# A gated MLP's last group in one phase of 512 tokens, with late products put off and TensorE's order written out

## The chip, the cores and the metric

One core of a Trainium2 chip runs the whole program. The time is the device time of one execution, in microseconds; the kernel before has a median of 612.99 us over 3 runs (610.72 to 613.15). The profile is of one execution, whose own time is 612.58 us and whose span, from the first to the last instruction, is 610.9 us. Engines are called as the profile calls them: PE is TensorE, PEld its weight loads, DVE is VectorE, ACT is ScalarE, POOL is GpSimd, SP issues most transfers.

## The reference

The program is three layers one after the other, on 1536 tokens of width 512, all in float32:

```
attn:  q, k, v (2, 8, 768, 64): each query sees the first 4 keys and the 128 keys up to its own; softmax
x    = attn with the heads side by side                       # (1536, 512)
mlp:   g = x @ w_gate;  x = (g / (1 + exp(-g)) * (x @ w_val)) @ w_out      # 512 -> 1536 -> 512
moe:   tokens with x @ w_skip > 0 are computed, the others are copied
       e = argmax(x @ w_gate2);  p = softmax(x @ w_gate2)[e]               # 8 experts
       out = x + p * (relu(x @ w1[e]) @ w2[e])                             # 512 -> 1024 -> 512
```

## The kernel before

Products that need more than TensorE's reduced float32 are split: a value is a rounded part and a rest (`hi` and `lo`, or `hh` and `hl`), and a product is three matmuls, hi by hi, hi by lo and lo by hi. ACT rounds (`act_copy`, line 71), and DVE or POOL takes the rest (`lo_of`, line 74).

Tokens go in 12 blocks of 128, three groups of four. Attention of a group runs between the MLP work of the group before. `PHASES` (line 38) lists the MLP's phases: group 0 and group 1 in one phase of 512 tokens each, group 2 in two phases of 256 tokens. A phase goes over the hidden layer in 12 chunks of 128. For each chunk `mlp` (line 571) projects to the gate and to the value (`proj`, 12 matmuls each, line 547), makes `th`, `hh` and `hl` on ACT and DVE, and then calls `down` (line 559) for the chunk before: three matmuls of 512 columns for each tile of 128 tokens, added up in a PSUM bank per tile (`acc`). The chunk's weights are split on the way (`prep`) into a ring of 12 buffers, anew in every phase.

After a group comes its routing. `take` copies a tile out of PSUM to `x2`, `turn` transposes it on PE (`x2t`, line 680), `logits` multiplies it by the gate weights (`lp`, line 688), and `choose` finds the expert and the row that each token gets in the buffer `xs` (small DVE operations, and the matmuls `rp` of lines 721 to 724), and scatters the rows there by indirect DMA from POOL's queue. For the groups listed in `APART` the gate sums come another way: `weigh` (line 692) multiplies a tile by one row of the gate weights on DVE, 36 times for a group, and `finish_apart` hands them out during the next phase. Before, this is group 0 alone.

`finish_last` ends the last phase. The tokens of expert 0 that were scattered before are loaded from `xs` as `xg`, and those of the last two tiles are put to them on PE, with one-hot matrices `at` (`start_x`, `put_in`, line 902), so that the first expert need not wait for the last scatter. Then `experts` goes over the 8 experts. An expert has a first block of 128 rows and, if it has more, a second of up to 64, under a branch: `block_h` and `few_h` (first layer, `hps`, lines 993 and 949), `turn_x` (transposes `xg`, line 934), `block_turn` and `few_turn` (transpose the hidden layer, `htp`), `block_y` and `few_y` (second layer, `yps`, lines 1019 and 975). `prep2` loads an expert's weights in pieces of four through 11 buffers called `stage` and splits them: ACT all four, POOL one rest, DVE three (`w<-stage,w` at line 74). `load_x` fetches an expert's rows when they have landed.

Each engine works its instructions off in the order in which they stand, one after the other. A scheduler puts them in that order when the program is built, on every engine, by the priority of the code's order and by what it takes to be ready.

Of the kernel before, what the change touches and what calls it, by code (L numbers as in the profile page):

```python
# [8 lines left out]
F32 = mybir.dt.float32  # L9
# [6 lines left out]
P = 128  # L16

@with_exitstack
def build(ctx: ExitStack, tc: tile.TileContext, q, k, v, n_sink, window,
# [53 lines left out]
    def lo_of(out, in_, hi, eng=None):  # L73
        (eng or nc.vector).tensor_tensor(out=out, in0=in_, in1=hi.bitcast(F32), op=ALU.subtract)  # L74
# [448 lines left out]
    LO = ["gvo", "", "", ""]  # L523
# [13 lines left out]
    hp = {}  # L537
    acc = {}
# [12 lines left out]
    def down(g, c, tiles, base=0):  # L551
        whi, wlo = wr["o", c]
        hh, hl = hp[c]
        for t in tiles:
# [3 lines left out]
            for m, (h_, w_) in enumerate(((hh, whi), (hh, wlo), (hl, whi))):  # L558
                nc.tensor.matmul(out=acc[g, t], lhsT=h_[:, s], rhs=w_, start=c == 0 and m == 0, stop=c == NFC - 1 and m == 2)  # L559
# [10 lines left out]

    def mlp(ph):
        g, t0, t1, c0, c1, _ = PHASES[ph]
        n = (t1 - t0) * P
        for c in range(c0, c1 + 1):
            if c < c1:
# [9 lines left out]
                act_copy(hh, th, 0.5)  # L585
                nc.vector.scalar_tensor_tensor(out=hl, in0=th, scalar=0.5, in1=hh.bitcast(F32), op0=ALU.mult, op1=ALU.subtract)  # L586
                hp[c] = (hh, hl)
                pace(ph, c)
# [71 lines left out]
    def route(pools, toks, rows, apart=None):  # L660
# [8 lines left out]
        def take(t, src):  # L669
            x2 = mo_.tile([P, RW], F32, tag="x2", name="x2", bufs=4)  # L670
            act_copy(x2[:, 0:DM], src)
# [5 lines left out]
        def turn(t):  # L677
# [4 lines left out]
            nc.vector.tensor_copy(x2T, tp)  # L682
# [12 lines left out]
        return take, turn, logits if apart is None else weigh, lambda meanwhile=None: choose(rt_, pa_ if apart is None else ps_, n, lp, [x2s[t] for t in range(n)], meanwhile)  # L695

    def choose(rt_, ps_, n, lp, x2s, meanwhile=None):
# [20 lines left out]
        if meanwhile:  # L718
            meanwhile[0]()
# [10 lines left out]
        if meanwhile:  # L730
            meanwhile[1](x2s, po)
# [97 lines left out]
    def finish_last(g, tiles, late):  # L829

        take, turn, logits, close = routing(g, tiles)
        n = len(tiles)
        a, b = NFC - 2, NFC - 1
        for c in (a, b):
            down(g, c, tiles[:-1], tiles[0])
        for i in range(n - 1):
            take(i, acc[g, tiles[i]])
        down(g, a, tiles[-1:], tiles[0])
# [531 lines left out]
```

## Time and profile before

| | |
|---|---|
| median of 3 runs | 612.99 us (610.72 to 613.15) |
| profiled execution | 612.58 us, span 610.9 us |
| PE busy | 578.4 us, 95% of the span, 3385 matmuls |
| DVE busy | 461.0 us, 75% |
| ACT busy | 369.3 us, 60% |
| POOL busy | 211.4 us, 35% |
| granted PE clock, mean | 0.979 of full speed |

PE's busy time is modelled for matmuls that overlap, so the distance from one matmul to the next says more than the duration of one. Times within the span are counted from its start. The last group's two phases begin at 331.17 us, the first expert's `hps` at 453.53 us, and the last matmul ends at 599.62 us.

### The profile page before, as it was taken

What the parts mean: (1) busy time and instruction counts of PE and PEld (TensorE: products, weight loads), DVE (VectorE), ACT (ScalarE), POOL (GpSimd) and SP (SyncE); (2) the same over time, 40 slices, a digit from 0 to 9 for tenths busy, and PEclk for the clock granted to TensorE, in tenths of its full rate; (3) what the DMA queues carried; (4) which work ended last, traced back from release to release, by engine and by line L of the source; (5) the groups of instructions that cost most, each with busy time, mean ns of one, the idle gap of its engine ahead of it and who ended that gap; (6) DMA issues with size and microseconds to landing.
All of it is one profiled execution on the core that took longest, in us unless ns stands there. A gap on an engine that the chain in (4) does not pass through costs nothing. (4 is left out here: it accounts for less than half of the span.)

```text
span 610.9 us, 10856 instructions
## 1 busy us (share of the span) xinstructions
PE 578.4 (95%) x3385; PEld 460.0 (75%) x3385; DVE 461.0 (75%) x1160; ACT 369.3 (60%) x864; POOL 211.4 (35%) x291
## 2 busy tenths in 40 slices
PE   7999999899999999999999999999997999999992
PEld 4556766677777777778788999889985787777771
DVE  4898898897657999976645676699657887988950
ACT  4888787876555664555543565575444766857720
POOL 3474362656543342322320300021034335545320
PEclk7999999899999999999999999999997999999997
DMA  8857889563212422000016000032029776969701
GB/s 200 216 141 182 235 248 257 167 208 57 83 16 35 131 38 67 12 19 1 17 44 217 30 1 0 35 116 70 1 79 324 248 242 210 344 205 307 279 7 33
DMA packets 89305, 78.22 MB, mean 128 GB/s; under 512 B 53371, under 2 KB 65659, under 8 KB 89234
## 3 DMA queue, kind: packets, MB, share of 16 engines
q1 hardware_dynamic: 86434, 71.71, 39.6%
q0 software_dynamic: 2512, 5.68, 2.8%
q8 instruction: 31, 0.51, 0.4%
q14 instruction: 40, 0.33, 0.2%
q10 hardware_dynamic: 288, 0.00, 0.0%
HBM read 67.73 MB, written 12.00 MB: 131 GB/s over the span
## 5 line engine op out<-in xcount | busy, mean ns | idle before, releaser
L547 PE MATMUL gv<-xt,ring 128*128 128x512 f32 (+1 forms) x1152 | 224.2, 345 | 0.9 <-DVE th L581 0.9
L547 PEld LDWEIGHTS gv<-xt,ring 128*128 128x128 f32 x1152 | 177.3, 189 | 28.8 <-issue 2.0
L71 ACT ACTIVATE ring<-w 128x512 fp32r<-128x512 f32 x144 | 90.1, 628 | 92.7 <-PE gv L547 70.0
L74 DVE TENSOR_TENSOR ring<-w,ring 128x512 fp32r<-128x512 f32 x108 | 75.3, 699 | 33.2 <-ACT ring L71 33.1
L74 DVE TENSOR_TENSOR w<-stage,w 128x512 fp32r<-128x512 f32 x96 | 88.7, 955 | 7.0 <-ACT w L71 4.1
L559 PE MATMUL acc<-ring,hh 128*128 128x512 f32 x288 | 92.5, 402 | 0.0
L71 ACT ACTIVATE w<-stage 128x512 fp32r<-128x512 f32 x128 | 73.1, 626 | 11.8 <-DMA stage<-in_moe_w_dram 9.0
L74 POOL TENSOR_TENSOR ring<-w,ring 128x512 fp32r<-128x512 f32 x36 | 49.2, 1368 | 52.2 <-ACT ring L71 47.8
L74 POOL TENSOR_TENSOR w<-stage,w 128x512 fp32r<-128x512 f32 x32 | 47.1, 1476 | 46.6 <-ACT w L71 23.6
L559 PEld LDWEIGHTS acc<-ring,hh 128*128 128x128 f32 x288 | 50.8, 188 | 11.5 <-issue 1.2
L559 PE MATMUL acc<-ring,hl 128*128 128x512 f32 x144 | 57.1, 398 | 0.0
L1019 PE MATMUL yps<-w,hT 128*128 128x512 f32 x192 | 47.1, 399 | 1.0 <-DVE w L74 0.6
L394 POOL TENSOR_SCALAR_AFFINE_SELECT pt<-pt 128x256 f32<-128x256 f32 x40 | 22.1, 554 | 71.9 <-ACT pt L71 71.9
L361 ACT ACTIVATE p<-p,st 128x132 f32<-128x132 f32 x96 | 38.2, 399 | 14.5 <-DVE st L357 13.6
L993 PE MATMUL hps<-w,xh 128*128 128x512 f32 x128 | 43.0, 415 | 0.8 <-PEq L1067 0.5
L1019 PEld LDWEIGHTS yps<-w,hT 128*128 128x128 f32 x192 | 35.3, 188 | 10.4 <-ACTq L1067 1.0
L745 POOL DMA_INDIRECT xs<-x,pi x12 | 12.7, 1060 | 85.4 <-DVE ring L74 49.3
L341 PE MATMUL s<-kq 64*128 64x260 f32 (+1 forms) x144 | 34.3, 408 | 2.6 <-DVE st L357 1.1
L71 ACT ACTIVATE hh<-th 128x512 fp32r<-128x512 f32 (+1 forms) x48 | 25.1, 524 | 19.0 <-DVE th L582 18.9
L582 DVE TENSOR_TENSOR th<-th,gv 128x512 f32<-128x512 f32 (+1 forms) x48 | 26.4, 551 | 11.7 <-PE gv L547 9.8
L559 PEld LDWEIGHTS acc<-ring,hl 128*128 128x128 f32 x144 | 27.0, 188 | 6.8 <-DVE hl L586 0.4
L581 DVE SCALAR_TENSOR_TENSOR th<-th,gv 128x512 f32<-128x512 f32 (+1 forms) x48 | 26.3, 548 | 7.3 <-ACT th L578 7.3
(192 smaller groups left out, 953.5 us busy)
## 6 DMA issues: line engine op xcount, KB each, us to landing
stage<-in_moe_w_dram SPq DMA_DIRECT2D x128, 256.0 KB, 4.5
st<-in_moe_w_gate_dram SPq DMA_DIRECT2D x12, 512.0 KB, 4.8
st<-in_moe_w_val_dram SPq DMA_DIRECT2D x12, 512.0 KB, 5.0
st<-in_moe_w_out_dram SPq DMA_DIRECT2D x12, 512.0 KB, 4.8
xs<-trash SPq DMA_DIRECT2D x8, 387.0 KB, 5.9
vb<-in_v_dram SPq DMA_DIRECT2D x12, 256.0 KB, 3.8
out_dram<-x SPq DMA_DIRECT2D x12, 256.0 KB, 2.8
wl<-wgt SPq DMA_DIRECT2D x4, 512.0 KB, 4.6
```

The source lines that it names most:

```text
L71: nc.scalar.activation(out=out, in_=in_, func=ACTF.Copy, scale=scale)
L74: (eng or nc.vector).tensor_tensor(out=out, in0=in_, in1=hi.bitcast(F32), op=ALU.subtract)
L341: m_ = nc.tensor.matmul(out=ss[h][:, 0:nk], lhsT=x_, rhs=y_, start=m == 0, stop=m == len(terms) - 1)
L361: nc.scalar.activation(out=p[:, h], in_=p[:, h], func=ACTF.Exp, scale=-1.0, bias=st[:, h:h + 1], accum_out=su[:, h:h + 1])
L394: nc.gpsimd.affine_select(out=d[:, 0], in_=d[:, 1], compare_op=ALU.is_ge, fill=0.0, base=0, pattern=[[0, 2], [1, P]], channel_multiplier=-1)
L547: nc.tensor.matmul(out=ps, lhsT=w_[:, kk * P:(kk + 1) * P], rhs=x_[:, kk, t0 * P:t1 * P], start=kk == 0 and m == 0, stop=kk == KD - 1 and ...
L559: nc.tensor.matmul(out=acc[g, t], lhsT=h_[:, s], rhs=w_, start=c == 0 and m == 0, stop=c == NFC - 1 and m == 2)
L581: nc.vector.scalar_tensor_tensor(out=th, in0=th, scalar=1.0, in1=gp, op0=ALU.add, op1=ALU.mult)
L582: nc.vector.tensor_tensor(out=th, in0=th, in1=vp, op=ALU.mult)
L745: d = nc.gpsimd.indirect_dma_start(out=xs[:, :], out_offset=bass.IndirectOffsetOnAxis(ap=pi[:, t], axis=0), in_=x2s[t], in_offset=None, bo ...
L993: nc.tensor.matmul(out=ps[half], lhsT=x_[:, kk, :], rhs=w_[:, kk, :], start=kk == 0 and m == 0, stop=kk == KD - 1 and m == 2)
L1019: nc.tensor.matmul(out=y, lhsT=h_[:, c, :], rhs=w_[:, c % 4, :], start=c == 0 and m == 0, stop=c == NF2 - 1 and m == 2)
```

## The change

- `PHASES`: group 2 is one phase of 512 tokens. Its weights are split once less; the chunks' matmuls have 512 columns and not 256.
- Of its 12 chunks, the last 8 are done for tiles 0 and 1 only (`KEPT`); for tiles 2 and 3 their `hh` and `hl` are kept in two buffers that the second group's tokens had, and their `down` comes late. The output weights of five chunks are split a second time for it (`next_o`).
- `finish_last` routes tiles 0 and 1 between these late matmuls, scatters them, and then routes tiles 2 and 3. Of the last tile the copies are halved between ACT and DVE.
- `APART` has group 1 too: its gate sums are 36 `weigh` on DVE during the last phase.
- `count_tokens` and `judge` move into the first expert's `block_h`; `block_h` takes a `middle`, in which the second block of the expert before is transposed; the order of the loads of `xg` and of the first expert's steps is another, and the buffer `xf` is there twice.
- From `finish_last` to the end of the experts PE's instructions stand as the code is written (`manual_schedule`); the other engines' are scheduled as before.

```diff
-    APART = (0,)
+    APART = (0, 1)
-    PHASES += [(2, 0, GB, 0, NFC, 3 * GS), (2, GB, GS, 0, NFC, 3 * GS)]
+    PHASES += [(2, 0, GS, 0, NFC, 3 * GS)]
+    KEPT = 8
...
-    def down(g, c, tiles, base=0):
+    def down(g, c, tiles, base=0, last=NFC - 1):
         whi, wlo = wr["o", c]
-        hh, hl = hp[c]
+        hh, hl = (kept if base else hp)[c]
...
+    def keep(c):
+        c -= NFC - KEPT
+        if c == 0:
+            kept["h"] = [xtp.tile([P, KEPT, GB * P], F32R, tag=f"xt{a}1", name=f"kept{a}") for a in range(2)]
+        return [a[:, c] for a in kept["h"]]
...
-            if ph == len(PHASES) - 1 and c >= c1 - 1:
-                if c == c1:
-                    return
-            elif c > c0:
-                down(g, c - 1, range(t0, t1), t0)
+            if last and c == c1:
+                down(g, NFC - 3, range(t0 + GB, t1), GB, NFC - 4)
+            if c > c0:
+                down(g, c - 1, range(t0, t0 + GB if last and c - 1 >= NFC - KEPT else t1), t0)
...
     def finish_last(g, tiles, late):
+        order = list(range(NFC - 3, NFC)) + list(range(NFC - KEPT, NFC - 3))
+        a, b = order[-2:]
+        again = order[3:]
...
+        take, turn, logits, close = routing(g, head)
+        for i in range(GB):
+            take(i, acc.pop((g, head[i])))
+        next_o()
+        late_down(order[1], tail)
+        turn(0)
+        next_o()
+        turn(1)
+        late_down(order[2], tail)
+        next_o()
+        logits(0)
+        late_down(order[3], tail)
+        next_o()
+        logits(1)
+        def ahead():
+            for c in order[4:-2]:
+                late_down(c, tail)
+                next_o()
+        close(None, ahead)
+        load_x(late, 0, 0)
+        take, turn, logits, close = routing(g, tail)
+        for c in (a, b):
+            late_down(c, tail[:-1])
+        take(0, acc[g, tail[0]])
+        for c in (a, b):
+            late_down(c, tail[-1:])
         turn(0)
...
+        take(1, acc[g, tail[1]], True)
+        turn(1, True)
+        logits(0)
+        logits(1)
+        close(lambda x2s, po: start_x(late, tp0, x2s, po), lambda: warm(12, acqp, "acq"))
...
     def start_x(late, tp, x2s, po):
+        put_in(tp, [(xg[0, 0], ident)], True)
+        warm(4, acqp, "acq")
...
+        def middle(e):
+            if e == 0:
+                count_tokens(attp)
+                judge()
+            elif e == 1:
+                few(0, few_h)
+                turn_x(1, 1)
+                with tc.issue_after(lows[0]):
+                    load_next(0)
+            else:
+                few(e - 1, few_turn)
...
-                block_h(e)
-                if e == 0:
-                    turn_x(0, 1)
+                block_h(e, lambda: middle(e))
...
+            if e == 0:
+                turn_x(1, 0)
+                for piece in range(2):
+                    prep2(late, 1, piece, anchors)
+                block_turn(0)
+                for piece in range(2, 4):
+                    prep2(late, 0, piece)
+                turn_x(0, 1)
+                continue
...
-            finish_last(g, range(t0, t1), late)
+            with tc.manual_schedule(engines={mybir.EngineType.PE}):
+                finish_last(g, range(t0, t1), late)
+                experts(late)
```

What this makes of the order is shown at three places. On PE, at the start of the last group (`x2t`, `lp` and `rp` are group 1's routing, `gv` the projections), there stood before:

```order
L559 MATMUL acc<-ring,hl 128x512
L680 MATMUL x2t<-ident,x_3873 128x128 x4
L680 MATMUL x2t<-ident,x_3878 128x128 x4
L547 MATMUL gv<-xt_2847,ring 128x256
L547 MATMUL gv<-xt_2848,ring 128x256
L547 MATMUL gv<-xt_2847,ring 128x256 x2
L688 MATMUL lp<-wgs,x2T 128x9 x4
L680 MATMUL x2t<-ident,x_3883 128x128 x4
```

and now there stands:

```order
L563 MATMUL acc<-ring,hl 128x512
L551 MATMUL gv<-xt_2847,ring 128x512
L551 MATMUL gv<-xt_2848,ring 128x512
L551 MATMUL gv<-xt_2847,ring 128x512 x2
L551 MATMUL gv<-xt_2848,ring 128x512
```

The transposes and logits of group 1 have left PE, and the projections follow the last `down` of group 1. At the end of the last group, PE now has the routing of tiles 0 and 1 (`lp`, `rp`) between late products (from `kept`):

```order
L714 MATMUL lp<-wgs,x2T 128x9 x4
L563 MATMUL acc<-ring,kept_4154 128x512 x2
L563 MATMUL acc<-ring,kept_4155 128x512
L563 MATMUL acc<-ring,kept_4154 128x512 x2
L563 MATMUL acc<-ring,kept_4155 128x512
L563 MATMUL acc<-ring,kept_4154 128x512 x2
L563 MATMUL acc<-ring,kept_4155 128x512
L563 MATMUL acc<-ring,kept_4154 128x512 x2
L563 MATMUL acc<-ring,kept_4155 128x512
L747 MATMUL rp<-seen,ones 128x18
L748 MATMUL rp<-oh,before 128x18
L750 MATMUL rp<-oh,ones 128x9
```

Twelve more late products and the routing of tiles 2 and 3 follow behind these rows. On DVE, in the first experts (`w` is a weight piece's rest, `h` the first layer's relu, `xf` the rest of a second block's tokens, for expert 0 and then for expert 1), there stood before:

```order
L997 TENSOR_SCALAR h_5328<-hps 128x512
L74 TENSOR_TENSOR xf<-xgt,xf 128x4x64
L74 TENSOR_TENSOR w_5471<-stage,w_5470 128x512
L1062 TENSOR_LOAD cnt
L1067 COMPARE_AND_BRANCH
L1067 UNCONDITIONAL_BRANCH x2
L74 TENSOR_TENSOR xl<-xgt,xh 128x512
L74 TENSOR_TENSOR w_5471<-stage,w_5470 128x512
L74 TENSOR_TENSOR xf<-xgt,xf 128x4x64
```

and now there stands:

```order
L77 TENSOR_TENSOR hT<-htp,hT 128x512
L77 TENSOR_TENSOR w_4997<-stage,w_4996 128x512
L77 TENSOR_TENSOR w_5015<-stage,w_5014 128x512 x3
L77 TENSOR_TENSOR xf<-xgt,xf 128x4x64
L1052 TENSOR_SCALAR h_5040<-hps 128x512
L1138 TENSOR_LOAD cnt
L1115 COMPARE_AND_BRANCH
L1115 UNCONDITIONAL_BRANCH x2
L77 TENSOR_TENSOR xf<-xgt,xf 128x4x64
```

Expert 1's `xf` stood behind 8 weight rests since the first `hps`; now it stands behind 12.

## Rows read from the trace of the kernel before

**Rows 1.** Windows: length, busy (count) PE PEld DVE ACT POOL, PEclk, DMA, GB/s
```profile
331.17:445.01 113.84, 112.97 (x809) 105.03 (x808) 83.38 (x185) 64.31 (x130) 11.01 (x16) 1.00 0.13 43
445.01:453.53 8.52, 8.47 (x73) 7.63 (x73) 4.47 (x24) 1.20 (x3) 1.19 (x2) 1.00 0.17 63
453.53:485.01 31.48, 27.93 (x127) 21.77 (x126) 25.06 (x35) 20.27 (x40) 13.69 (x12) 0.89 0.81 263
485.01:599.62 114.61, 109.85 (x561) 87.15 (x559) 93.82 (x131) 70.90 (x137) 49.70 (x41) 1.00 0.68 224
```

**Rows 2.** PE's timeline, group 1's end: start, us, engine, line, operation, count
```profile
319.97 5.75 PE L547 MATMUL gv<-xt,ring 128*128 128x512 f32 x24
325.56 0.63 PE L559 MATMUL acc<-ring,hh 128*128 128x512 f32 x2
...
331.17 1.04 PE L680 MATMUL x2t<-ident,x 128*128 128x128 f32 x8
```

**Rows 3.** Windows: eight half-chunks of 256 tokens, 24 projections and 6 down products each
```profile
353.29:387.34 34.05, 34.05 (x241) 31.74 (x240) 24.64 (x49) 20.71 (x40) 0.00 (x0) 1.00 0.00 1
```

**Rows 4.** PE's timeline, group 1's routing
```profile
332.55 1.06 PE L688 MATMUL lp<-wgs,x2T 128*128 128x9 f32 x8
333.46 0.63 PE L680 MATMUL x2t<-ident,x 128*128 128x128 f32 x4
333.94 0.96 PE L688 MATMUL lp<-wgs,x2T 128*128 128x9 f32 x8
334.75 0.64 PE L680 MATMUL x2t<-ident,x 128*128 128x128 f32 x4
```

**Rows 5.** Gate sums on DVE: line 692 (ns min/median/max), and a window amid them
```profile
L692 DVE CUSTOM_DVE_ANT_0 wl<-x,wl x36: 641/682/774, 200.1 to 262.3; 128x512 f32<-128x512 f32 x36
...
220.00:230.00 10.00, 10.00 (x52) 7.66 (x51) 10.00 (x36) 6.37 (x18) 3.38 (x7) 1.00 0.21 33
```

**Rows 6.** The page's groups: busy us, mean ns | idle before, releaser
```profile
L547 PE MATMUL gv<-xt,ring 128*128 128x512 f32 (+1 forms) x1152 | 224.2, 345 | 0.9 <-DVE th L581 0.9
```

**Rows 7.** PE's timeline, from the last down product to the first expert
```profile
445.01 0.62 PE L680 MATMUL x2t<-ident,x 128*128 128x128 f32 x4
...
450.25 0.40 PE L722 MATMUL rp<-oh,before 128*128 128x18 f32 x2
...
451.73 2.05 PE L902 MATMUL xgt<-at,x 128*128 128x128 f32 x16
```

**Rows 8.** Last scatter: POOL, SP's queue, and DMA issues (count, KB, us to landing)
```profile
451.40 0.19 POOL L732 CAST pi<-po 128x2 int32<-128x2 f32 x1 [32.74 <-DVE po L728]
...
456.46 2.11 SPq L891 DMA_DIRECT2D xg<-xs  x4
...
xg<-xs SPq DMA_DIRECT2D x3, 258.0 KB, 2.5
```

**Rows 9.** PE's timeline, first experts; in brackets the idle time before and its releaser
```profile
460.12 0.46 PE L934 MATMUL xgt<-ident,xg 64*128 64x64 f32 x4 [0.76 <-DMA xg<-xs]
...
463.56 0.69 PE L934 MATMUL xgt<-ident,xg 64*128 64x64 f32 x4 [1.36 <-DVE xf L74]
464.17 2.07 PE L993 MATMUL hps<-w,xh 128*128 128x512 f32 x4
...
471.39 3.95 PE L949 MATMUL hps<-w,xf 128*128 128x512 f32 x16 [0.32 <-ACT w L71]
475.18 0.63 PE L993 MATMUL hps<-w,xh 128*128 128x512 f32 x2
...
478.19 5.86 PE L1019 MATMUL yps<-w,hT 128*128 128x512 f32 x24
```

**Rows 10.** Windows: the stretch of expert 1's first products
```profile
464.17:469.30 5.13, 5.13 (x18) 4.18 (x18) 4.40 (x6) 2.56 (x5) 1.59 (x1) 0.52 1.04 344
```

**Rows 11.** DVE: weight rests, timeline at the first, and their group from 455 to 582
```profile
455.27 3.69 DVE L74 TENSOR_TENSOR w<-stage,w 128x512 fp32r<-128x512 f32 x3 [0.61 <-ACT w L71]
...
L74 DVE TENSOR_TENSOR w<-stage,w 128x512 fp32r<-128x512 f32 x87 | 79.9, 952 | 7.0 <-ACT w L71 4.1 <-DVEq L1085 1.1 <-DMA stage<-in_moe_w_dram 0.6
```

More of the change, by code (lines that the diff above doesn't have):

```diff
@@ L558, in down @@
             for m, (h_, w_) in enumerate(((hh, whi), (hh, wlo), (hl, whi))):
-                nc.tensor.matmul(out=acc[g, t], lhsT=h_[:, s], rhs=w_, start=c == 0 and m == 0, stop=c == NFC - 1 and m == 2)
+                nc.tensor.matmul(out=acc[g, t], lhsT=h_[:, s], rhs=w_, start=c == 0 and m == 0, stop=c == last and m == 2)
     steps = [(ph, c) for ph, p in enumerate(PHASES) for c in range(p[3], p[4])]
@@ L573, in mlp @@
         n = (t1 - t0) * P
+        last = ph == len(PHASES) - 1
         for c in range(c0, c1 + 1):
@@ L667, in route, with copy, take @@
         x2s, turned = {}, {}
-        def take(t, src):
+        def copy(out, in_, halves):
+            if halves:
+                m = out.shape[1] // 2
+                nc.vector.tensor_copy(out[:, m:], in_[:, m:])
+                act_copy(out[:, 0:m], in_[:, 0:m])
+            return halves
+        def take(t, src, halves=False):
             x2 = mo_.tile([P, RW], F32, tag="x2", name="x2", bufs=4)
-            act_copy(x2[:, 0:DM], src)
+            if not copy(x2[:, 0:DM], src, halves):
+                act_copy(x2[:, 0:DM], src)
             x2s[t] = x2
@@ L681, in turn @@
             x2T = mo_.tile([P, KD, P], F32, tag="th", name="x2T")
-            nc.vector.tensor_copy(x2T, tp)
+            if not copy(x2T, tp, halves):
+                nc.vector.tensor_copy(x2T, tp)
             turned[t] = x2T
@@ L693, in weigh, with choose @@
                                            accum_out=lp[:, 16 * t + e:16 * t + e + 1])
-        return take, turn, logits if apart is None else weigh, lambda meanwhile=None: choose(rt_, pa_ if apart is None else ps_, n, lp, [x2s[t] for t in range(n)], meanwhile)
-    def choose(rt_, ps_, n, lp, x2s, meanwhile=None):
+        return take, turn, logits if apart is None else weigh, lambda meanwhile=None, ahead=None: choose(rt_, pa_ if apart is None else ps_, n, lp, [x2s[t] for t in range(n)], meanwhile, ahead)
+    def choose(rt_, ps_, n, lp, x2s, meanwhile=None, ahead=None):
         lg = lp[:, 0:16 * n].rearrange("p (t e) -> p t e", e=16)
@@ L983, in few_y, with block_h @@
         put_row(o, xg[e, 1], put_out)
-    def block_h(e):
+    def block_h(e, middle):
         xh, xl = xgT[e, 0]
@@ L994, in block_h @@
                                      start=kk == 0 and m == 0, stop=kk == KD - 1 and m == 2)
-        for half in range(2):
             nc.vector.tensor_scalar(out=h2[e, 0][half], in0=ps[half], scalar1=0.0, scalar2=None, op0=ALU.max)
+            if half == 0:
+                middle()
     def block_turn(e):
@@ L1046, in experts, with load_next, few @@
         rv = {}
-        for e in range(2):
-            for b in range(2):
-                load_x(late, e, b)
+        for e, b in ((1, 0), (0, 1), (1, 1), (0, 0)):
+            load_x(late, e, b)
         for piece in range(2):
             prep2(late, 0, piece)
+        def load_next(e):
+            if e + 2 < NE:
+                for b in range(2):
+                    load_x(late, e + 2, b)
+        def few(e, part):
+            with tc.If(rv[e] > P):
+                part(e)
+        def middle(e):
[9 more added lines that the diff above has]
+                few(e - 1, few_turn)
         for e in range(NE + 1):
@@ L1077, in experts @@
                     prep2(late, e, piece)
-            if e > 0:
-                with tc.If(rv[e - 1] > P):
-                    few_y(e - 1)
-            if e + 2 < NE:
-                for b in range(2):
-                    load_x(late, e + 2, b)
-            if e < NE:
-                with tc.If(rv[e] > P):
-                    few_turn(e)
+            few(e - 1, few_y)
+            load_next(e)
     def general():
```

71 lines of the change are left out of this document (31 added, 40 removed).

## The prediction

> **What bounds the kernel now.** I read the windows first, one for each stage that the change touches [rows 1]. PE is busy for 112.97 of 113.84 us from the start of the last group to its last down product, and nearly all the time in the three stages behind; its weight loads run beside it, DVE is the next with 83.38, and comes near it only in the experts, with 93.82 of 114.61 us. So time is to be had by taking matmuls off PE, by hiding what PE waits for, and little else. PE's timeline then shows what it does in these stretches [rows 2, 4, 7, 9], and the timelines of DVE, POOL and SP's queue show the chains that it waits for [rows 8, 11]. The reader is to see a PE that is full up to 445.01, a routing of 8.52 us with a chain of small steps in it, and then a stretch from 453.53 to 485.01 with 3.5 us of idle time and a clock of 0.89: the one place where PE waits for much.
>
> Stages before 331.17 keep their instructions in their order. I cost them at nothing.
>
> **The last group's products.** With 512 columns, 24 projections take from 319.97 to 325.56 and 24 down products from there to 331.17: 11.20 us for 48, 0.233 us each [rows 2]. One phase of 512 tokens has 12 x 24 projections and 12 x 12 down products, 432 in all, 100.8 us. Before, eight half-chunks take 34.05 us, 4.256 each [rows 3], so 24 take 102.1. This gains 1.3 us.
>
> A rule speaks of the same term. The Trainium skill (TensorE: Matmul & The Clock Gate, "Wait — 56ns, not 53.3ns?") has a warm matmul take its columns at 2.4 GHz and some 2.5 ns more; by that, joining two matmuls of 256 columns gives back only 2.5 ns, over 288 pairs 0.7 us (an estimate from that page), and the forecast would be 602.4. This trace does not agree: its steps are larger at either width (0.233 us, and 0.119 for a half-chunk's projections), and it decides.
>
> **Group 1's gate sums.** They leave PE: 16 transposes, of which four take 0.48 us (333.46 to 333.94), and four logits, 0.91 us (332.55 to 333.46) for the first and 0.81 (333.94 to 334.75) for each other [rows 4]. That is 1.9 + 3.3 = 5.2 us. On DVE 36 sums come in, at 0.682 us [rows 5]: 24.6 us. DVE has 83.38 us of work in a stretch that becomes some 105 us long [rows 1]; of the second splitting 36 weight rests go and five come again, 31 operations of the sums' own shape, 21 us if they cost as much. So DVE stays near 80%. In the window from 220 to 230 DVE was full, gate sums of group 0 in it, and PE was full too [rows 5]. I cost the sums at nothing; if DVE got behind, PE would wait for the `th` that frees a projection's bank.
>
> **Routing of tiles 0 and 1.** Its PE work (8 transposes, 2 logits, `rp`; some 3.2 us) is in both versions. Before, PE filled its waits with the next phase's projections, now with late products; no gain. The waits of `gv` for `th`, 0.9 us in the whole trace [rows 6], may go with the scattered order around it.
>
> Up to the last down product the sum is 1.3 + 5.2 + 0.9 = 7.4. Adding up what the new order holds instead (100.8, then 1.0 for group 1's `rp` and 3.2 for the routing) gives 105.0 against 113.84: 8.8. The difference is in small gaps of the old order, which the new one may or may not have. I take 8.3, and keep 7.4 and 8.8 as ends.
>
> **From the last down product to the first expert.** This takes 8.52 us before [rows 1], along transposes, logits, DVE's small steps, `rp` at 450.25, the one-hot products at 451.73 and the first `hps` at 453.53 [rows 1, 7]. All of it remains. Halved copies may give 0.5. But expert 0's earlier rows come later: the scatter of tiles 0 and 1 now runs just before. In the last scatter, from `rp` (450.25) to the loads' issue (456.46) took 6.2 us, and a load lands 2.5 us after [rows 7, 8]; 8.7 in all. Between the new `rp` of tiles 0 and 1 and the place where PE wants these rows lie 2.8 us of late products (12 x 0.233) and the 5.2 us from 445.01 to 450.25, and a 0.6 for `rp` itself: 8.6. The two meet. I take 0, with ends of a gain of 0.5 and a loss of 2 (a scatter that is held up on POOL).
>
> **First experts.** From the first `hps` to expert 0's `yps` it takes 24.66 us (453.53 to 478.19) [rows 1, 9]. PE waits there for DMA and DVE, its clock falls to 0.52 for 5.13 us [rows 10], and `few_h` begins at 471.39, 17.86 us after the first `hps`. In the new order `few_h` needs expert 1's `xf` from DVE, which stands behind 12 weight rests. DVE began them 1.74 us after the first `hps` (455.27). At 0.95 us each [rows 11], 12 take 11.4; around them stand three relus, two `hT`, an `xl`, two `xf` and small steps, some 4.7. That makes 17.9: `few_h` begins when it did. But behind it stood nine products of expert 1 (475.18 on, 2.1 us), which are now ahead of it. So `yps` comes 3.8 (`few_h`) and 0.9 (transposes) later, at 22.6: a gain of 2.0. Ends: with the first three's 1.23 us for all (3.69 / 3), 14.8 + 6.4 = 21.2, and a loss of 1.3; were DVE free, PE's own row of work (48 products, 11.2, transposes and the one wait for a relu, together some 16.3) ends it at 21.0, a gain of 3.6.
>
> **Later experts.** Their work is the same. PE is idle for 4.8 of 114.61 us [rows 1]. Earlier relus and transposes inside `block_h` may save a little; I take 0.5, with ends of 2 gained and 2 lost. On SP the first experts' weight loads now stand ahead of the output rows and of the loads of `xg`, in a stretch with DMA busy for 0.13 of the time [rows 1]: nothing.
>
> **Sum.** 8.3 + 0 + 2.0 + 0.5 = 10.8 off the profiled execution's 612.58 (its span of 610.9 and 1.7 around it): 601.8. The median is 0.4 above that execution, within the spread of the three runs.
>
> **Rivals.**
> - *DVE lets go early.* Weight rests come at the shorter of their times, and PE's clock does not fall. First experts gain 3.6 and the products 8.8, later ones 2, the halves 0.5: 597.7. For it: the first three rests take 1.23 each and all 87 of them 0.95 in the mean [rows 11], so some are much shorter. Against it: POOL has as many rests to take as before, at the same time.
> - *Gain given back behind the products.* The scatter of tiles 0 and 1 lands 2 us late, DVE takes 1.23 us for each rest (1.3 lost), later experts lose 2 as PE has got ahead of DVE's weights: 612.58 - 8.3 + 5.3 = 609.6 at worst, 606.9 with half of it. For it: DVE is busy for 25.06 of 31.48 and 93.82 of 114.61 us in the experts [rows 1]. Against it: half of the terms would have to fall badly at once.
> - *The written order stalls (slower).* The scheduler could put products that were ready ahead of an instruction that had to wait; written out, every instruction that waits holds all of PE. A wait costs its length each time in experts 1 to 7. From 10.3 / 7, 1.5 us in each, the products' and the start's gains are gone; with 2.2 us in each the time is 612.58 - 10.3 + 15.4 = 617.7. For it: PE did wait 1.36 us for an `xf` [rows 9]. Against it: between an expert's first layer and the transposes of it the code has a `block_y` of 24 products, 5.6 us of cover.
> - *Nothing gained by the sums.* DVE with 36 sums and expert 0's rests holds up the projections for as long as PE saved on them, 5.2 us, and the first experts gain nothing: 612.58 - 8.3 + 5.2 = 609.5. Against it stands the full window [rows 5].
>
> **How the numbers follow.** Forecast 0.54 (its own range 598 to 605), early DVE 0.15, gain given back 0.20, the sums 0.06, the written order 0.05. A measurement of this kernel tells 0.5% from no change, 3.1 us here. Faster by more (below 609.9): all of the first two, nine tenths of the third and some of the fourth, 0.88; within it 0.08; slower 0.04. The range reaches from 596 (a little below early DVE) to 608 (into the gain given back); what is left out is the slow case, the worst of the third, and the far side of early DVE, under 0.2.
>
> **What would show it.** In the new profile: one 512-column projection every 0.233 us from 331.17 on, with no wait of `gv` for `th`; the last down product near 436.7; the first `hps` some 8.5 us behind it, with the transposes of `xg` waiting under 1 us for their load; DVE without a gap from there to the second `xf`, and `few_h` waiting for that `xf`; expert 0's `yps` some 22.6 us behind the first `hps`; PE idle for about 4 us from expert 2 on. The forecast is wrong if `gv` waits for `th` in every chunk, if the first `hps` comes more than 10.5 us behind the last down product, or if PE waits over 1 us in each later expert.

## The result and the profile after

The changed kernel takes 607.61 us in the median of 8 runs (606.38 to 610.63), the kernel before 612.05 on the same chip (8 runs, 610.49 to 613.88). The ratio is 0.9914, with a 95% interval of 0.9888 to 0.9940: 5.3 us faster by the ratio (4.4 by the medians), where 10.8 were forecast. The profiled execution took 606.38 us, with a span of 604.7. A second set of runs of the changed kernel gave a ratio of 0.9884 (0.9846 to 0.9922).

The windows of the four stages of the changed kernel answer to [rows 1] (columns as there). The third ends at expert 0's `yps`, which was at 478.19 before [rows 9].

```profile
331.70:436.76 105.06, 105.06 (x474) 85.45 (x473) 78.30 (x192) 43.51 (x83) 8.41 (x13) 1.00 0.24 79
436.76:446.25 9.49, 8.10 (x71) 7.54 (x70) 4.04 (x21) 1.37 (x4) 3.42 (x7) 1.00 0.46 157
446.25:472.36 26.11, 21.81 (x98) 16.51 (x96) 21.28 (x34) 16.98 (x33) 10.39 (x10) 0.87 0.87 288
472.36:592.68 120.32, 116.39 (x591) 92.78 (x590) 97.57 (x135) 72.99 (x144) 49.68 (x42) 1.00 0.65 218
```

Set against before, stage by stage: the last group 113.84 to 105.06, 8.78 gained; from there to the first `hps` 8.52 to 9.49, 0.97 lost; on to expert 0's `yps` 24.66 to 26.11, 1.45 lost; from there to the last matmul 121.43 (478.19 to 599.62) to 120.32, 1.11 gained. The group begins 0.53 us later (331.70 and 331.17) with nothing changed ahead of it, and from the last matmul to the end of the span it is 12.02 us, not 11.28: 0.74 lost. The sum, 8.78 - 0.97 - 1.45 + 1.11 - 0.53 - 0.74 = 6.20, is the difference of the two spans.

PE's timeline at the start of the last group answers to [rows 2]:

```profile
331.70 11.34 PE L551 MATMUL gv<-xt,ring 128*128 128x512 f32 x48
342.88 0.62 PE L563 MATMUL acc<-ring,hh 128*128 128x512 f32 x2
```

and the page's group of the projections to [rows 6] (busy us, mean ns, idle before them):

```profile
L551 PE MATMUL gv<-xt,ring 128*128 128x512 f32 x864 | 216.9, 401 | 0.0
```

Here 48 projections take 11.18 us, 0.233 each, and no projection waits in the whole trace (0.0 at the end of the last row, 0.9 before).

PE's timeline from the routing of tiles 0 and 1 (`rp`) to the first experts, in brackets the idle time before and its releaser, answers to [rows 7, 9]:

```profile
433.45 0.38 PE L748 MATMUL rp<-oh,before 128*128 128x18 f32 x2
...
443.14 1.13 PE L957 MATMUL xgt<-ident,xg 128*128 128x128 f32 x8 [0.63 <-issue]
444.11 0.60 PE L505 MATMUL warm<-ident 128*128 128x256 bf16 x4
444.55 1.95 PE L957 MATMUL xgt<-at,x 128*128 128x128 f32 x16
446.25 0.71 PE L1050 MATMUL hps<-w,xh 128*128 128x512 f32 x2
...
453.27 0.65 PE L991 MATMUL xgt<-ident,xg 128*128 128x128 f32 x4 [0.98 <-DVE cnt L786]
453.76 0.60 PE L1064 MATMUL htp<-ident,h 128*128 128x128 f32 x4
456.96 1.12 PE L1064 MATMUL htp<-ident,h 128*128 128x128 f32 x4 [2.60 <-DVE xl L77]
...
467.65 3.95 PE L1006 MATMUL hps<-w,xf 128*128 128x512 f32 x16 [0.43 <-PEq L1115]
...
472.36 5.86 PE L1076 MATMUL yps<-w,hT 128*128 128x512 f32 x24
```

Three things are new. Expert 0's earlier rows (`xgt<-ident,xg`) are waited for, and the one-hot products stand behind them and behind four fillers (0.44 us, 444.11 to 444.55). The next transposes wait 0.98 us for `cnt`, the count of the experts' tokens, which the change put into the first expert and which PE loads there for its branches. And the second transpose of the hidden layer (`htp` at 456.96) waits 2.60 us for an `xl` on DVE, which it doesn't read: the two transposes and that `xgt` share two PSUM banks. From there on four transposes take 1.12 us, not 0.60, and the granted clock is 0.50, the lower level (1.2 GHz), from 456.25 to 461.25, as it was 0.52 before [rows 10]. (`cnt` ended at 452.34, 0.93 us before PE went on. In all ten profiles of this kernel and its variants in which PE waits there, it goes on 0.93 to 0.97 us behind the end of `cnt`; one of them, three_mended, gives the load, `DMA xg<-xs`, as the releaser.)

DVE's timeline in that stretch answers to [rows 11]:

```profile
447.99 3.67 DVE L77 TENSOR_TENSOR w<-stage,w 128x512 fp32r<-128x512 f32 x3 [0.62 <-ACT w L74]
...
452.19 0.15 DVE L786 CAST cnt<-cp 128x8 int32<-128x8 f32 x1
452.26 1.82 DVE L77 TENSOR_TENSOR w<-stage,w 128x512 fp32r<-128x512 f32 x1
...
454.96 0.68 DVE L1052 TENSOR_SCALAR h<-hps 128x512 f32<-128x512 f32 x1
...
456.23 0.68 DVE L77 TENSOR_TENSOR xl<-xgt,xh 128x512 fp32r<-128x512 f32 x1
...
464.94 0.42 DVE L77 TENSOR_TENSOR xf<-xgt,xf 128x256 fp32r<-128x256 f32 x1 [0.71 <-ACT xf L74]
```

The `cnt`, the second relu (454.96) and the `xl` (456.23) stand behind weight rests; the last row is expert 1's `xf`. And SP's queue:

```profile
440.40 9.85 SPq L946 DMA_DIRECT2D xg<-xs  x5
450.34 29.22 SPq L928 DMA_DIRECT2D stage<-in_moe_w_dram  x31
```

The weights' transfers go on at 450.34, 13.58 us behind the last product. Before it was 13.66 (458.67 and 445.01).

### The profile page after: what moved, and what is told of

Its sections match the earlier page's. It is cut to its first block, busy times and chain, and to the rows that moved or that the text cites. A ratio compares the mean times of both kernels' runs of the same rounds, so it can differ in the third digit from the quotient of the medians.

```text
span 604.7 us, 10096 instructions
## 1 busy us (share of the span) xinstructions
PE 569.9 (94%) x3049; PEld 440.3 (73%) x3049; DVE 456.1 (75%) x1170; ACT 347.8 (58%) x818; POOL 206.7 (34%) x291
## 5 line engine op out<-in xcount | busy, mean ns | idle before, releaser
L551 PE MATMUL gv<-xt,ring 128*128 128x512 f32 x864 | 216.9, 401 | 0.0
L551 PEld LDWEIGHTS gv<-xt,ring 128*128 128x128 f32 x864 | 158.1, 188 | 38.3 <-issue 2.0
L74 ACT ACTIVATE ring<-w 128x512 fp32r<-128x512 f32 x113 | 70.8, 629 | 94.9 <-PE gv L551 72.4
L563 PE MATMUL acc<-ring,hh 128*128 128x512 f32 x256 | 82.5, 403 | 0.0
L77 DVE TENSOR_TENSOR ring<-w,ring 128x512 fp32r<-128x512 f32 x77 | 54.0, 701 | 26.7 <-ACT ring L74 26.7
L718 DVE CUSTOM_DVE_ANT_0 wl<-x,wl 128x512 f32<-128x512 f32 x72 | 50.2, 697 | 1.1
L563 PE MATMUL acc<-ring,hl 128*128 128x512 f32 x128 | 50.9, 398 | 0.0
L594 DVE TENSOR_TENSOR th<-th,gv 128x512 f32<-128x512 f32 x36 | 24.5, 681 | 14.4 <-PE gv L551 14.3
L175 DVE SCALAR_TENSOR_TENSOR w<-w,st 128x512 int32<-128x512 int32 x36 | 30.2, 839 | 2.3 <-ACT w L170 1.0
L344 PEld LDWEIGHTS s<-kq 64*128 64x128 f32 x144 | 16.9, 196 | 20.5 <-issue 10.5
```

The lines of the kernel that those rows point to most:

```text
L74: nc.scalar.activation(out=out, in_=in_, func=ACTF.Copy, scale=scale)
L77: return (eng or nc.vector).tensor_tensor(out=out, in0=in_, in1=hi.bitcast(F32), op=ALU.subtract).ins
L175: nc.vector.scalar_tensor_tensor(out=di, in0=di, scalar=3, in1=low, op0=ALU.logical_shift_left, op1=ALU.bitwise_or)
L344: m_ = nc.tensor.matmul(out=ss[h][:, 0:nk], lhsT=x_, rhs=y_, start=m == 0, stop=m == len(terms) - 1)
L551: nc.tensor.matmul(out=ps, lhsT=w_[:, kk * P:(kk + 1) * P], rhs=x_[:, kk, t0 * P:t1 * P], start=kk == 0 and m == 0, stop=kk == KD - 1 and ...
L594: nc.vector.tensor_tensor(out=th, in0=th, in1=vp, op=ALU.mult)
```

## The experiments

Each is the changed kernel with one edit, if not said otherwise. All of them, ratios against the kernel before, stages in us, each from its own profile:

| kernel | ratio (95%) | last group | last product to first hps | first hps to yps of expert 0 | last product to last matmul |
|---|---|---|---|---|---|
| before | 1 | 113.84 | 8.52 | 24.66 | 154.61 |
| changed | 0.9914 (0.9888-0.9940) | 105.06 | 9.49 | 26.11 | 155.92 |
| again | 0.9884 (0.9846-0.9922) | 105.06 | 9.69 | 26.49 | 156.48 |
| sums_on_pe | 0.9998 (0.9971-1.0026) | 110.45 | 8.87 | 25.22 | 156.69 |
| experts_scheduled | 0.9900 (0.9861-0.9939) | 105.07 | 9.64 | 17.87 | 158.84 |
| head_earlier | 0.9870 (0.9829-0.9911) | 105.07 | 8.39 | 26.42 | 155.41 |
| wait_filled | 0.9894 (0.9858-0.9930) | 105.07 | 9.42 | 27.04 | 156.21 |
| wait_away | 0.9854 (0.9819-0.9889) | 105.06 | 12.02 | 22.81 | 156.35 |
| no_pool_rests | 0.9889 (0.9864-0.9913) | 104.93 | 9.57 | 24.00 | 154.73 |
| old_experts | 0.9931 (0.9908-0.9955) | 105.05 | 12.24 | 22.63 | 161.90 |
| bank_alone | 0.9861 (0.9807-0.9915) | 105.07 | 9.76 | 24.20 | 155.77 |
| relu_alone | 0.9902 (0.9871-0.9933) | 105.07 | 9.78 | 25.17 | 156.96 |
| three_mended | 0.9828 (0.9777-0.9879) | 105.09 | 8.38 | 26.70 | 157.31 |
| four_mended | 0.9878 (0.9833-0.9923) | 105.09 | 12.94 | 24.48 | 157.12 |

**The same kernel again.** 

> The changed kernel once more, as it is. In its first profile the last group began 0.53 us later than in the profile of before, though nothing ahead of it is different, and from the last matmul to the end it took 12.0 us against 11.3. Theory A: these 1.3 us are the scatter of single executions, so that the start of the last group lies anywhere from 331.0 to 331.9 and the end piece from 11.2 to 12.1 us; the stages between repeat to 0.2 us: 105.1 us to the last down product, 9.5 from there to the first hps, 26.1 from there to expert 0's yps. Rival: the change itself costs them (its larger late buffers, another state of the queues), and both repeat. Ratio to the kernel before 0.991 again.

Theory A holds: the stages repeat to 0.4 us, the group to 0.01, and the whole from the last product to the last matmul to 0.56. In the fourteen profiles the last group begins between 328.3 and 334.7 us, and the piece behind the last matmul is 11.2 to 12.5; the scatter ahead of the group is wider than was expected. So 1.3 us of the difference of the first two spans say nothing of the change.

**Group 1's sums on TensorE.** 

> The changed kernel with group 1's gate sums on TensorE again (group 1 taken out of the list of groups with sums on VectorE), all else as changed. Theory A (the sums were worth what they take on TensorE, and VectorE bears them for nothing): the last group takes 5.2 us longer, 110.3 and not 105.1, the stages behind are the same, and the time rises by 5.2 us, to a ratio of 0.9999. Rival B (the 36 sums made VectorE late with the experts' weights, and the first experts pay for it): the last group takes 5.2 us longer, but the first hps to expert 0's yps falls from 26.1 to 24 or less, and the time rises by 3 us or less.

```diff
-    APART = (0, 1)
+    APART = (0,)
```

```profile
329.51:439.96 110.45, 110.45 (x521) 90.58 (x520) 60.85 (x126) 43.61 (x83) 9.70 (x13) 1.00 0.11 37
```

The window of the last group: 5.39 us longer (5.2 expected), DVE 17.45 us less busy, the ratio 0.9998 (0.9999 expected). First `hps` to `yps` is 0.9 shorter, not 2, and the 155.92 to the last matmul become 156.69. So A, not B: the sums are worth their time on PE, and DVE bears them.

**Experts ordered by the scheduler.** 

> The changed kernel, but with TensorE's order written out only as far as the first expert's tokens; in the experts the scheduler orders TensorE, as it did before the change. Theory A (in the first experts TensorE waits because VectorE is late with rests and transposes, whatever order TensorE has): first hps to expert 0's yps stays within 1 us of 26.1, the time within 1.5 us of the changed kernel. Rival C (the written order holds TensorE up: products that are ready stand behind a waiting instruction): the waits of 2.6 and 0.98 us are filled with products of expert 1, first hps to expert 0's yps falls to 23.5 or less, and the time by 2 us or more, ratio 0.988 or less.

```diff
             with tc.manual_schedule(engines={mybir.EngineType.PE}):
                 finish_last(g, range(t0, t1), late)
-                experts(late)
+            experts(late)
```

The scheduler does draw products ahead: expert 0's `yps` begins 17.87 us behind the first `hps`, where C said 23.5 or less. But it is given back, at the transposes of expert 2's hidden layer,

```profile
496.09 0.55 PE L1064 MATMUL htp<-ident,h 128*128 128x128 f32 x3 [2.79 <-DVE xl L77]
```

and the last matmul comes 158.84 us behind the last product, 2.4 to 2.9 later than in the two profiles of the changed kernel, although the clock stayed at 1.00 through all the experts. C falls: without the written order the time is no lower (0.9900, against 0.9914 and 0.9884 with it). Theory A's bound of 1.5 us on the time is less than these ratios can tell apart; its 1 us at `yps` does not hold.

**Rows of tiles 0 and 1 placed earlier.** 

> The changed kernel with the rows of tiles 0 and 1 placed one late chunk earlier (six late products moved from ahead of their placing to behind it, 1.4 us), and without the four filler matmuls between the two parts of expert 0's tokens (0.44 us). Theory A (from the last product to the first hps it took 9.5 us since expert 0's earlier rows landed late and the one-hot products had to stand behind them): the transposes of these rows no longer wait 0.63 us, the first hps comes 8.4 to 8.6 us behind the last down product, and all behind it 1.0 us earlier; time 1.0 lower, ratio 0.990. Rival D (the chain through logits, choice, and one-hot matrices sets the first hps, the rows are covered anyway): 9.0 us or more, a gain of 0.4 at most, which is the fillers'. Rival E (the placing has to wait for the choice, which the six products covered): TensorE waits there for VectorE by up to 1.4 us, and the time is no lower.

```diff
-            for c in order[4:-2]:
+            for c in order[4:5]:
...
-        for c in (a, b):
+        for c in order[5:]:
...
-        warm(4, acqp, "acq")
```

```profile
433.83 4.44 PE L563 MATMUL acc<-ring,kept 128*128 128x512 f32 x18
...
443.73 1.14 PE L957 MATMUL xgt<-ident,xg 128*128 128x128 f32 x8
444.70 2.03 PE L957 MATMUL xgt<-at,x 128*128 128x128 f32 x16
446.49 0.71 PE L1049 MATMUL hps<-w,xh 128*128 128x512 f32 x2
```

PE's timeline: 18 late products behind the placing, not 12; the rows are there without a wait (0.63 before the edit), and the first `hps` is 8.39 us behind the last product. A is shown (0.44 of the 1.10 us are the fillers'), D and E fall. At the last matmul 0.5 us of it is left against the first profile of the changed kernel (155.41 and 155.92) and 1.1 against the second (156.48): two profiles of one kernel differ by half of the gain.

**The wait filled.** 

> The changed kernel with 24 filler matmuls (0.107 us each, 2.57 in all) on TensorE between the two transposes of expert 0's hidden layer, where it waited 2.60 us and its clock then fell to 0.50. Theory A1 (VectorE, with the weights' transfers behind it, sets the pace of the experts up to expert 1's yps; what TensorE gains ahead of that it gives back there): the clock stays at 1.00, first hps to expert 0's yps falls from 26.1 - 26.5 to 25.0, but TensorE then waits over 1 us at the transposes of expert 2's hidden layer, 47 us behind the first hps, and from the first hps to the last matmul it stays 146.4 to 146.8 us. Theory A2 (TensorE sets the pace, and what the half clock costs is lost for good): first hps to the last matmul falls by 1.2 to 2.9 us, to 143.5 - 145.4, the time with it.

```diff
         for half, h in enumerate(h2[e, 0]):
+            if e == 0 and half:
+                warm(24, acqp, "acq")
             turn_h(hT[e, 0], h, half)
```

The 2.60 us are gone, and 6 us further on PE waits 2.15 us for an `hT` on DVE; the clock, full until 460, is 0.83 from 460 to 470. First `hps` to last matmul is 146.79 us, as A1 expected, but 27.04 to `yps` is what neither expected, and the wait at expert 2's transposes that A1 named is not there (from 470 on no wait of PE is over 0.8 us). What the clock's fall alone costs, this did not tell.

**The wait taken away.** 

> The changed kernel with that wait itself taken away: the tokens of expert 1 and of expert 0's second block are transposed into the fillers' PSUM banks, so that the second transpose of the hidden layer needs no bank that VectorE has yet to empty, and ScalarE makes the second half's relu of expert 0, which stood behind four weight rests on VectorE. Theory A1 (VectorE sets the pace to expert 1's yps): the wait of 2.60 falls below 0.6, expert 1's first products then wait for VectorE instead, and first hps to the last matmul changes by less than 0.8 (one relu less on VectorE). Theory A2 (the missed bank and its wait cost the first experts what was missing): first hps to expert 0's yps comes to 23.5 or less, nearer the 22.6 that were forecast, and first hps to the last matmul to 143.5 or less; ratio 0.984.

```diff
-        tp = attp.tile([P, KD, P], F32, tag="att", name="xgt")[:, :, 0:n]
+        pool, tag = (acqp, "acq") if e + b == 1 else (attp, "att")
+        tp = pool.tile([P, KD, P], F32, tag=tag, name="xgt")[:, :, 0:n]
...
+            if e == 0 and half:
+                nc.scalar.activation(out=h2[e, 0][half], in_=ps[half], func=ACTF.Relu)
```

PE's timeline, and the windows up to the first `hps` and from there to `yps`:

```profile
454.50 1.04 PE L1068 MATMUL htp<-ident,h 128*128 128x128 f32 x8
...
465.09 3.95 PE L1007 MATMUL hps<-w,xf 128*128 128x512 f32 x16 [1.06 <-DVE xf L77]
```

```profile
434.97:446.99 12.02, 11.26 (x72) 10.33 (x70) 4.19 (x21) 1.36 (x4) 3.41 (x7) 0.72 0.41 146
446.99:469.80 22.81, 19.33 (x98) 14.61 (x96) 19.69 (x32) 17.01 (x33) 10.65 (x10) 1.00 0.91 289
```

Eight transposes in one piece, no fall of the clock behind them, and `yps` at 22.81 us: A2's side there. `few_h` now waits for `xf`, and begins 18.10 us behind the first `hps`. From the first `hps` to the last matmul it is 144.33 us, 2.1 and 2.5 less than in the two profiles of the changed kernel (146.43 and 146.78): more than the 0.8 that A1 allowed, and short of A2's 143.5. But in this execution the clock fell ahead of the first `hps` (0.72 in the first window, 12.02 us for what took 9.49), so that what stands behind it had 2.5 us more to get ready, and from the last product to the last matmul it is 156.35 us, as in the changed kernel (155.92 and 156.48). One profile can't tell whether the gain would have lasted without that fall. The ratio, 0.9854 where A2 named 0.984, leans to A2.

**Its two halves.** 

> The changed kernel with the fillers' PSUM banks for the two transposes of tokens behind the first hps, and nothing else (VectorE keeps the relu). Theory A2 (the second transpose of expert 0's hidden layer waited 2.60 us for a bank that VectorE's xl had to empty, 10.7 us behind the first hps): it now waits for the relu alone, which ended 9.4 us behind the first hps, so that the wait falls to 1.2 - 1.5 us, and if the clock stays, first hps to expert 0's yps falls to 24 us. Rival J (the relu, which stands behind weight rests, was what it waited for): the wait stays 2.3 us or more.

> The changed kernel with ScalarE's relu for the second half of expert 0 and nothing else (the banks as they were). Theory A2: the bank still holds the transpose up until VectorE's xl, which comes one relu (0.6 us) earlier, so that the wait falls from 2.60 to 1.9 - 2.1 us and no further. Rival J (the relu was the cause): the wait falls below 0.6 us, as with both edits.

The edits are the first and the second part of the diff above. The second transpose with the banks changed, and with the relu moved:

```profile
454.39 0.66 PE L1065 MATMUL htp<-ident,h 128*128 128x128 f32 x4 [1.33 <-DVE h L1053]
```

```profile
453.88 0.66 PE L1067 MATMUL htp<-ident,h 128*128 128x128 f32 x4 [2.60 <-DVE xl L77]
```

With the banks the wait falls to 1.33 and has the relu as its releaser; with the relu alone it stays 2.60. So the bank was what held it up (A2), and J's condition that the relu alone would end it falls. The 1.9 to 2.1 expected of the relu did not come, as `xl` stayed where it was, 10.0 us behind the first `hps`: a weight rest took the relu's place on DVE.

**No rests on GpSimd.** 

> The changed kernel with the four weight rests that GpSimd takes for the first two experts (two pieces of expert 0, two of expert 1) on VectorE too. In the profile a rest took VectorE 0.6 us one behind the other, and 1.2 to 1.8 where GpSimd took one at the same time. Theory F (the two hold each other up, so that a rest on GpSimd saves VectorE nothing): VectorE's 16 rests take 0.6 to 0.7 us each, some 10 us, against 15 for 12 of them now; first hps to expert 0's yps falls by 1.5 us or more. Rival (they are slow for another reason, the weights' transfers or ScalarE): the rests keep 1.0 us and more, VectorE has 4 more of them, and first hps to expert 0's yps grows by 2 us or more.

```diff
-                l_ = lo_of(lo[:, a], st, hi[:, a], nc.vector if a else nc.gpsimd)
+                l_ = lo_of(lo[:, a], st, hi[:, a], nc.vector if a or (e, piece) in ((1, 0), (1, 1), (0, 2), (0, 3)) else nc.gpsimd)
```

```profile
447.57 2.50 DVE L77 TENSOR_TENSOR w<-stage,w 128x512 fp32r<-128x512 f32 x4
```

DVE's first four rests take 2.50 us, where three had taken 3.67. All 16 up to expert 1's `xf` take 11.3 us; the 12 of the changed kernel had taken 10.6, not the 15 of the expectation. F holds for the first experts: 24.00 us to `yps`, 2.1 less. The wait for `cnt` is gone, and the one for the bank has become shorter, as DVE comes to its `xl` sooner, 7.35 us behind the first `hps` and not 9.98:

```profile
454.45 0.66 PE L1064 MATMUL htp<-ident,h 128*128 128x128 f32 x4 [1.18 <-DVE xl L77]
```

So the slow rests had a part in both waits. From the last product to the last matmul, 154.73 is the least of all the changed kernels. In the times (0.9889) it can't be told from the changed kernel.

**The experts of before.** 

> The changed kernel up to the first expert's tokens, with the experts of before (their order of transposes, loads and branches, one second-block buffer, TensorE's order from the scheduler). Theory A1 (the new order of the experts neither gave nor cost much, as VectorE and the weights' transfers set their pace): first hps to the last matmul 145.5 to 146.8 us (146.1 before, 146.4 and 146.8 changed), the time within 1 us of the changed kernel. Rival G (the new order costs the first experts 1.5 to 1.8 us by itself): first hps to expert 0's yps goes back to 24.7, first hps to the last matmul is below 145.2, and the time 1.5 lower. Rival H (the new order was needed behind the new last group, as the rows of the first tiles land later there): first hps to the last matmul 148 or more.

The edit puts the old `experts` and `block_h`, shown in the diff of the change, in the place of the new ones. The first `hps` to the last matmul takes 149.7 us (447.57 to 597.23), which is H's sign, and neither A1's nor G's. But in this profile the clock fell three times (439 to 449, 455 to 460 and 490 to 500), two of them all in that stretch, so that it does not show that the new order is needed behind the new last group. What the new order is worth is not settled: 5.4 to 6.0 us from the last product by this profile, 1.0 and 2.9 us by the ratios, whose interval (0.9908 to 0.9955) overlaps with both of the changed kernel's.

**The edits together.** 

> The changed kernel with the earlier placing of tiles 0 and 1 (8.39 us from the last product to the first hps, where it was 9.49), the fillers' banks and ScalarE's relu (first hps to expert 0's yps 22.81, where it was 26.11) together. If the two add up: 8.4 us and 22.8 us where the clock stays at 1.00, first hps to the last matmul 144.3, or 147.1 with a fall of the clock in them; from the last product to the last matmul 152.7 (155.9 changed, 154.6 before), the time 3.2 below the changed kernel, ratio 0.984. If VectorE and the weights' transfers set the pace (theory A1), the 1.1 us gained ahead of the first hps come back as waits in experts 1 and 2, and from the last product to the last matmul it stays above 153.8.

> The same three and the four weight rests of the first two experts on VectorE, not GpSimd. With them alone first hps to expert 0's yps came to 24.00 and VectorE's 16 rests took no longer than 12 had. If the gain adds to the others, first hps to expert 0's yps is 22.3 or less and the time 0.5 below the three's. If with the bank's wait gone VectorE is the one that is waited for (the second blocks' xf, 18 us behind the first hps), the 4 rests more make it later: first hps to expert 0's yps is 23.3 or more, and the time not below the three's.

PE's, DVE's and ACT's timelines of the three:

```profile
461.82 0.43 PE L991 MATMUL xgt<-ident,xg 64*128 64x64 f32 x4 [0.30 <-PEq L1118]
...
468.66 5.46 PE L1006 MATMUL hps<-w,xf 128*128 128x512 f32 x16 [3.42 <-DVE xf L77]
```

```profile
468.11 0.41 DVE L77 TENSOR_TENSOR xf<-xgt,xf 128x256 fp32r<-128x256 f32 x1
```

```profile
464.30 1.18 ACT L74 ACTIVATE w<-stage 128x512 fp32r<-128x512 f32 x2 [1.53 <-DMA stage<-in_moe_w_dram]
```

The 8.4 us came, the 22.8 didn't: `few_h` waits 3.42 us for its `xf`, which stands on DVE behind weight rests; these wait for ACT, and ACT waits for the transfers. To the last matmul it is 157.31 us, over the 153.8 that A1 named. With the fourth edit it is 24.48 to `yps` (23.3 or more was the sign of a DVE that is waited for; the wait of 3.34 us at `few_h` is put down to ACT's rounded weights there) and 157.12, and the time is not below the three's. The profile of the three is of an execution of 610.07 us, where the median of their runs is 605.14. Their interval (0.9777 to 0.9879) lies below that of the changed kernel's first set of runs (0.9888 to 0.9940) and overlaps with that of the second (0.9846 to 0.9922): that a version is faster than the changed kernel was not shown for certain.

## Why the forecast came out as it did

The measured 607.61 us lies in the stated range, 0.4 us from its end, and above the forecast's own 598 to 605: it is inside because the range was drawn into the rival *gain given back*. What the forecast said held for the last group, and not for the two stages behind it.

**Last product, forecast 8.3 off, measured 8.78.** Right, step by step: 0.233 us for each of the products, no wait of `gv`, and 5.4 us for the sums by the experiment (5.2 forecast). The small gaps of the old order went too, which was the upper end. That it came at 436.76, where 436.7 was named, is luck: the group gained 0.5 us more than forecast and began 0.53 later.

**Last product to first `hps`, forecast 0, measured a loss of 0.97.** The two chains were seen to "meet", and it was inside the end of 2. The rows' chain was sized too short: from `rp` (433.45) to the issue of the load (440.40) it took 6.95 us, where 6.2 was taken from the last scatter, and the four fillers stood in no sum. By head_earlier the loss is the rows' late landing and what stood in line behind it.

**First experts, forecast a gain of 2.0, measured a loss of 1.45.** This step failed, beyond its own worse end of 1.3. It had PE's own row of work end ahead of DVE's, 16.3 us behind the first `hps` with "the one wait for a relu", so that `few_h` waits for DVE's `xf`. In the changed kernel `few_h` began at 21.4 us (467.65), 2.3 us after that `xf` had ended. The sum counted the instructions that stand ahead on each engine, and not the PSUM banks nor the count that PE loads: PE waited 0.98 us for `cnt` and 2.60 for a bank, and then ran at 0.50. DVE's part was nearer: the second `xf` ended 19.1 us behind the first `hps` (forecast 17.9), and the 12 rests took 10.6 us (forecast 11.4). In wait_away `few_h` does wait for the `xf`, at 18.10, and `yps` is at 22.81, where 22.6 was forecast; but there the first `hps` came 2.5 us late itself. With the banks changed and no fall of the clock ahead of the first `hps` it is 24.20 (bank_alone) and 26.70 (three_mended), at a clock of 0.93 and 0.94, so the agreement is in part luck.

**Later experts, forecast 0.5, measured 1.11.** Within its ends.

In the profiles, mending the two losses did not bring their time back. Windows from the last product to the last matmul (154.61 us before), changed, bank_alone and three_mended:

```profile
436.76:592.68 155.92, 146.31 (x755) 116.83 (x753) 122.90 (x189) 91.34 (x180) 63.49 (x59) 0.98 0.68 226
451.76:471.76 20.00, 15.70 (x67) 11.60 (x65) 16.86 (x29) 11.16 (x22) 6.94 (x7) 0.83 0.95 318
```

```profile
435.17:590.94 155.77, 145.56 (x755) 115.97 (x753) 125.79 (x189) 91.38 (x180) 63.38 (x59) 0.99 0.69 226
```

```profile
439.80:597.11 157.31, 144.89 (x751) 115.64 (x749) 125.26 (x188) 92.59 (x181) 63.31 (x57) 0.99 0.68 222
454.80:474.80 20.00, 14.74 (x68) 11.10 (x68) 13.40 (x24) 10.32 (x21) 6.09 (x6) 0.91 1.02 338
```

From the changed kernel to three_mended PE's busy time falls from 146.31 to 144.89 us, 0.44 of it the fillers that are gone, and its idle time rises from 9.6 to 12.4: here the waits that are mended come back as others. In the 20 us from 15 us behind the last product the DMA engines are busy for 0.95 of the time in the changed kernel and 1.02 in three_mended. The weights' transfers go on 13.6 to 13.9 us behind the last product before, in the changed kernel and in three_mended (458.67, 450.34 and 453.67), behind the loads of `xg`, for which SP's queue stands until the last scatter is over. A first `hps` that comes earlier brings neither the weights nor their rests earlier. In three_mended PE has transposed expert 1's second block 22.0 us behind the last product (461.82), in the changed kernel 27.0 us behind it (463.80), and the `xf` made of it ends 28.7 and 28.6 us behind it: a PE that is 5 us ahead does not get it sooner. That supply sets the pace there fits all of these rows; that earlier transfers would free it was not tried, and stays open.

The times lean the other way. The four versions with the banks changed have ratios of 0.9828 to 0.9878, each below both of the changed kernel (0.9914 and 0.9884), and relu_alone, which leaves the bank as it was, has 0.9902. But head_earlier, which leaves it too, has 0.9870, and most of the intervals overlap. So some of the time may have come back in executions that no profile shows, and this too stays open.

Of the rivals, *gain given back behind the products* came nearest (606.9 with half of it): the rows did land late, and the first experts lost more than it had, through the count and a bank that were waited for. Slow rests had a part in these waits, as no_pool_rests shows, though the 12 rests took 0.89 us each in the mean and not 1.23. The later experts lost nothing. *The written order stalls* did not come: in the later experts PE is idle for 3.9 of 120.32 us, where that rival needed 1.5 in each, and experts_scheduled is not faster. *Nothing gained by the sums* is refuted by sums_on_pe.

## What to carry to other kernels

Where an order is written out, count the buffers as well as the instructions: a transpose can wait for a bank that another engine has yet to empty, though it needs nothing of what is in it. Count the values that an engine loads for its branches, too: they are made on another engine, behind whatever stands there. Before forecasting that an earlier start is kept, look at what the transfers behind it wait for. And forecast the stages behind a gain as a whole, since waits moved from one place to the next in these profiles, and set the times of several executions beside a profile, which is of one.

## What was not expected of the hardware

**A rest on DVE waits out a whole one on GpSimd.** Of the changed kernel, GpSimd's timeline:

```profile
452.24 1.27 POOL L77 TENSOR_TENSOR w<-stage,w 128x512 fp32r<-128x512 f32 x1
```

DVE's rest began at 452.26 and took 1.82 us: GpSimd's ended at 453.51, and 0.57 us later DVE's did, which is about the 0.62 that one takes in no_pool_rests. The Trainium skill (SBUF — State Buffer, "Who interferes with whom") has a VectorE instruction with two inputs from SBUF contend with a GpSimd one that reads there, and the one that comes second stand until the first is done; this row agrees. So where the two meet, a rest given to GpSimd costs DVE up to 1.2 us (1.82 less 0.62), twice what it takes off it.

**The clock falls in different places of the same instructions.** From the last product to the first `hps` wait_away and the changed kernel have the same instructions on TensorE, after the same 105.06 us of full work, and the same wait of 0.56 or 0.57 us for `x`. In the one the granted clock of that stage was 0.72, in the other 1.00 (and 0.87 in the next). It fell there in three of the fourteen profiles, at a cost of 2.5 us and more (12.02 for 9.49, and 12.94 for 8.38 in four_mended), and in one (experts_scheduled) not at all before the end of the experts. A stage's gain of 1 to 2 us can't be read from one profile unless the clock's row stands beside it.
